# A third buffer for a head's queries and keys, for the first nine of 64 heads, in memory that the mixer's hidden tiles take later

## The chip, the cores and the metric

One core of a Trainium2 chip. The metric is the device time of one execution in microseconds (us); lower is better. The engines are TensorE (PE: matmuls, and PEld for its weight loads), VectorE (DVE), ScalarE (ACT), GpSimd (POOL) and SyncE (SP), which issues the transfers here. Each runs its own instructions in program order and waits for the others by semaphores.

## The reference, cut to what matters

Causal attention in blocks of 64 over 8 batches of 8 heads, 576 positions of 64 features each, then a mixer on the joined heads:

```python
scores = scale * np.matmul(q, k.transpose(0, 1, 3, 2))   # q, k, v: (8, 8, 576, 64)
scores = np.where(mask, scores, -1e9)                    # block_i >= block_j
attn = np.exp(scores - scores.max(-1, keepdims=True))
attn = attn / (attn.sum(-1, keepdims=True) + 1e-9)
out = np.matmul(attn, v)                                 # heads joined: x, (8, 576, 512)
u = x + ((x.transpose(0, 2, 1) @ U) @ V).transpose(0, 2, 1)
return u + np.maximum(u @ w_ch1, 0.0) @ w_ch2            # 512 -> 2048 -> 512
```

## The kernel before, in words

**Order of the work.** Nothing is written in program order. Each piece of work is added to a plan as a task: an engine, an estimated duration, a priority, the buffers it reads and writes. When all tasks are known, `issue` walks through the time that these estimates make and gives each engine, whenever it is idle there, the ready task with the lowest priority number whose PSUM banks are free. That walk fixes the order of the instructions on every engine; on the chip each engine keeps that order and waits where an estimate was off. So one changed dependency can move tasks on all engines, before and after the place itself.

**Heads.** Head `h` has priority `1000 * h` and a little. Its queries and keys are one transfer of 288 KB into a buffer `raw` (`split_qk`, issued at L886, or in two pieces at L889 for head 0): 64 partitions of features, 576 columns of queries, 576 of keys. The other 64 partitions hold constants that add the mask, filled once at the start (L828 to L836). ACT scales the keys in place (L902). `raw` is a ring of two, so head `h` takes `raw[h % 2]`, and its transfer has to wait until all the score products of head `h - 2` have read that buffer. The task of head `h + 1` has priority `1000 * h - 900`, ahead of the work of head `h`.

**Softmax of a head.** The 576 queries are five tiles. Tile 4 is the widest and has a double bank of its own (`bw`, only one); tile 3 takes one of two banks `bf` for heads below 8; tiles 2, and 1 with 0, take banks of the four `ba`, leaving at least one. The products are L962 in full fp32 for heads below 12 (L966 and L967 after that), DVE takes the maximum (L980), ACT the exponential (L991) into `p`, DVE and POOL normalise (L1007, L1008, L1017), PE transposes (L1050), ACT or DVE copies to `pw` for heads below 10 (L1027, L1025), PE multiplies by V (L1093). Every second head `mix` adds the low-rank part (L1134 to L1168) and stores `u` (L1173).

**Weights and mixer.** In the same stretch the mixer's first weights arrive as 64-bit words, 512 KB at a time (L372, L387), and are put together to fp32 by ACT and DVE (L353, L331, L332, L337, L345) and split in two parts (L360, L361). When the first block's eight heads are through and the first weights stand, mixer products (L465, L488) fill TensorE between the heads. After the attention, later weights and products in another scheme (L659) go on to the end.

**Memory.** The pool `ep` holds `pw`, which only heads below 10 use. Its room is given up by a task `hidden` once these heads are done, and taken over by `hh` and `hl`, the results of the ReLU.

Of the kernel before, what the change touches and what calls it, by code (L numbers as in the profile page):

```python
# [9 lines left out]
F32 = mybir.dt.float32  # L10
# [6 lines left out]
P = 128  # L17
S = 576
# [119 lines left out]
class Plan:  # L138
# [8 lines left out]
    def add(self, engine, ns, prio, fn, reads=(), writes=(), hold=(), after=0, port=False):  # L147

        n = len(self.tasks)
        deps = set()  # L150
        for b in reads:
            deps.update(b.writers)
            b.readers.append(n)
        for b in hold:
            deps.update(b.readers, b.writers)
        for b in writes:
            deps.update(b.readers, b.writers)
            b.writers, b.readers = [n], []
        deps.discard(n)
        slots = {b for b in (*reads, *writes) if b.pool is not None}  # L160
        for b in slots:
            b.users += 1
        self.tasks.append((engine, ns, prio, fn, deps, after, slots, port or engine == "POOL"))
# [76 lines left out]
def _act(n, sbuf=False):  # L240
    return (93 if sbuf else 52) + 0.833 * n


def _dve(n):
    return 69 + 1.042 * n


def _pe(*ns, m=()):

    m = [*m, *[P] * len(ns)][1 : len(ns)] + [P]  # L250
    return sum(max(0.85 * w, n * COL) for n, w in zip(ns, m))
# [3 lines left out]
def attention_then_mixer(  # L255
# [21 lines left out]
    def f32(ap):  # L277
        return ap.bitcast(F32)
# [6 lines left out]
    ap = actx.enter_context(tc.tile_pool(name="ap", bufs=1))  # L285
    ep = ectx.enter_context(tc.tile_pool(name="ep", bufs=1, side="right"))

    def buf(pool, shape, dtype, name):
        return Buf(pool.tile(shape, dtype, name=name))

    def ring(pool, n, shape, dtype, name):
        return [buf(pool, shape, dtype, f"{name}{i}") for i in range(n)]
# [500 lines left out]

    q2_r = ring(ap, 2, [P, S], F32R, "q2_")
    k2_r = ring(ap, 2, [P, S], F32R, "k2_")
    raw_r = ring(ap, 2, [P, 2 * S], F32, "raw")
    ss_r = [b.split(5) for b in ring(ap, 2, [P, 5, 2], F32, "ss")]

    pt_r = [ring(ap, PB[i], [P, P * (i + 1)], F32, f"p{i}_") for i in range(5)]
# [2 lines left out]
    def transposed(pool, dtype, name):  # L802
        return [
            buf(pool, [P, _at(g, NK[g] - 1).stop], dtype, f"{name}{g}").split(len(BLOCKS[g])) for g in range(2)
        ]

    pw_r = [transposed(ep, F32, f"pw{n}") for n in range(2)]
    q1_r = ring(ap, 2, [P, S], F32R, "q1_")
    k1_r = ring(ap, 2, [P, S], F32R, "k1_")
# [69 lines left out]
            )  # L879

    def split_qk(h, pr):
        raw, q1, k1, q2, k2 = (r[h % 2] for r in (raw_r, q1_r, k1_r, q2_r, k2_r))

        def fetch():
            if h:
                nc.sync.dma_start(out=raw[0:64, :], in_=qk[h])  # L886
            else:
                for a in (S, 0):
                    nc.sync.dma_start(out=raw[0:64, a : a + S], in_=qk[h, :, a : a + S])  # L889

        if h in (FS - 2, FS - 1):

            for n, (x, o) in enumerate(((q2, 0), (k2, S))):
                add(
                    "DVE", _dve(S) / 2, pr, lambda x=x, o=o: nc.vector.tensor_copy(x[64:P, :], raw[64:P, o : o + S]),
                    [raw], [x],
                )
        add("SP", 820, pr, fetch, writes=[raw], after=DL)
        if h < FS:
            add(  # L900
                "ACT", _act(S, True), pr,
                lambda: nc.scalar.activation(raw[0:64, S : 2 * S], raw[0:64, S : 2 * S], AF.Copy, scale=SCALE), [raw], [raw],  # L902
            )
            return
        top = slice(0, 64)
        add("ACT", _act(S, True), pr, lambda: nc.scalar.copy(q2[top], raw[top, 0:S]), [raw], [q2])
        add(
            "ACT", _act(S, True), pr,
            lambda: nc.scalar.activation(raw[top, S : 2 * S], raw[top, S : 2 * S], AF.Copy, scale=SCALE), [raw], [raw],
        )  # L910
        add("ACT", _act(S, True), pr, lambda: nc.scalar.copy(k1[top], raw[top, S : 2 * S]), [raw], [k1])
        add("POOL", 1380, pr, lambda: nc.gpsimd.tensor_sub(q1[top], raw[top, 0:S], f32(q2[top])), [raw, q2], [q1])  # L912
        add("POOL", 1380, pr, lambda: nc.gpsimd.tensor_sub(k2[top], raw[top, S : 2 * S], f32(k1[top])), [raw, k1], [k2])  # L913

        add("SP", 600, pr, lambda: nc.sync.dma_start(out=f32(q1[64:P]), in_=f32(q2[top])), [q2], [q1], after=DL)
        add("SP", 600, pr, lambda: nc.sync.dma_start(out=f32(k1[64:P]), in_=f32(k1[top])), [k1], [k1], after=DL)
# [20 lines left out]
    def softmax(h, tiles, pr):  # L937

        q1, k1, q2, k2, ss, mx = (r[h % 2] for r in (q1_r, k1_r, q2_r, k2_r, ss_r, mx_r))
        raw = raw_r[h % 2]  # L940
        wide = 4 in tiles
        bank = Buf(pool=banks_w if wide else banks_f if h < 8 and tiles[0] == 3 else Rest(banks_a))

        parts, at = [], 0
        for i in tiles:
            parts.append((i, at))
            at += P * i + 64

        def view(i, at):
            return bank[:, :, :T] if wide else bank[: P if i else 64, at : at + P * i + 64]  # L950

        def products():
            for i, at in parts:
                qs = slice(P * i + 64 - (P if i else 64), P * i + 64)
                for j in range(2 if wide else 1):
                    o = bank[:, j, :T] if wide else view(i, at)
                    ks = slice(j * T, j * T + T) if wide else slice(0, P * i + 64)
                    if h < FS:
                        if not i:

                            o, qs = bank[:, at : at + 64], slice(0, P)
                        nc.tensor.matmul(  # L962
                            o, raw[:, qs], raw[:, S + ks.start : S + ks.stop], start=True, stop=True
                        )
                        continue
                    nc.tensor.matmul(o, q1[:, qs], k1[:, ks], start=True, stop=False)  # L966
                    nc.tensor.matmul(o, q2[:, qs], k2[:, ks], start=False, stop=True)  # L967

        ns, ms = [], []
        for i in tiles:  # L970
            ns += [T] * 4 if wide else [P * i + 64] * 2
            ms += [P if i else 64] * (4 if wide else 2)
        if h < FS:
            add("PE", sum(1.667 * n for n in ns) / 2, pr, products, [raw], [bank])
        else:
            add("PE", _pe(*ns, m=ms), pr, products, [q1, k1, q2, k2], [bank])
        for i, at in parts:
            add(
                "DVE", _dve(P * i + 64), pr,
                lambda i=i, at=at: nc.vector.tensor_reduce(  # L980
                    out=mx[: P if i else 64, i : i + 1], in_=view(i, at), op=ALU.max, axis=AX.XY if wide else AX.X,
                    negate=True,
                ),
                [bank], [mx.parts[i]],
            )
        for i, at in parts:
            pt, rows = pt_r[i][h % PB[i]], P if i else 64

            def exponentials(i=i, at=at, pt=pt, rows=rows):
                out = pt[:rows, : P * i + 64]  # L990
                nc.scalar.activation(  # L991
                    out.rearrange("p (j k) -> p j k", j=2) if wide else out, view(i, at), AF.Exp,
                    bias=mx[:rows, i : i + 1], accum_out=ss[:rows, i, 0:1],
                )

            add(
                "ACT", _act(P * i + 64) + 188, pr, exponentials, [bank, *(mx.parts[i] for i in tiles)],
                [pt, ss.parts[i]],
            )
# [182 lines left out]

    wa = weight_tiles(wp, 0)
    split_qk(0, 0.0)
    split_v(0, 2.0)
    mixing_weights(MP)
# [32 lines left out]
            for n, b in enumerate(whole):  # L1219
                b.ap = t[:, 2 * n : 2 * n + 2, :]  # L1220

    early = [b for x in pw_r for y in x for b in y.parts]
    add("SP", 0, -1.0, hidden, early, hh_r + hl_r, hold=early)

    for n in range(2):
# [44 lines left out]
```

## Time and profile before

| | |
|---|---|
| median of 3 runs | 1182.55 us (1182.36 to 1183.16) |
| profiled execution | 1182.37 us, of which 1180.6 us are the profile's span |
| TensorE | busy 1164.1 us, 99% of the span |
| VectorE, ScalarE, GpSimd | 79%, 66%, 38% of the span |

The span starts with the first instruction of the profile and ends with the last; the 1.8 us around it are in the device time. A busy TensorE is a union of modelled instruction intervals, which overlap. A piece of the chain of work is the instruction that held up what came next.

### The profile page before, as it was taken

The page shows a single profiled execution, that of the slowest core. Times are in us where ns is not written, and L with a number is a line of the kernel's source. Part 1 is how long each engine was busy: PE and PEld are TensorE (multiplying, and loading weights), DVE is VectorE, ACT ScalarE, POOL GpSimd, SP SyncE. Part 2 cuts the span into 40 slices and gives each one's busy share as a digit, 9 for nine tenths or more (in the row PEclk, how much of TensorE's full clock was granted, in tenths as well). Part 3 has the DMA queues.
Part 4 walks back from the last instruction along what each step waited for, and adds up shares of the span by engine and source line. Part 5 has one row for each costly group of instructions (what it writes and reads, how often), then busy time and mean ns, then how long its engine had stood idle before and what let it go on. Part 6 is the DMA issues. An engine that isn't in the chain of part 4 may idle for free.

```text
span 1180.6 us, 25204 instructions
## 1 busy us (share of the span) xinstructions
PE 1164.1 (99%) x8988; PEld 1131.4 (96%) x8988; DVE 936.2 (79%) x2009; ACT 774.9 (66%) x1924; POOL 451.2 (38%) x582
## 2 busy tenths in 40 slices
PE   9989999999999999999999999999999999999998
PEld 7778999999999999999999999999999999999998
DVE  6898887877887877777877587327989889889887
ACT  7888888989888888898887342114544444444443
POOL 5556876676757666766674122110000000000000
PEclk9999999999999999999999999999999999999999
DMA  4445565433433433443331434211132132132121
GB/s 142 141 153 154 160 177 140 116 115 108 114 112 110 123 105 111 114 117 110 112 94 52 142 113 145 66 52 50 61 122 71 51 121 70 53 121 62 60 81 41
DMA packets 75884, 122.69 MB, mean 104 GB/s; under 512 B 8944, under 2 KB 52976, under 8 KB 75760
## 3 DMA queue, kind: packets, MB, share of 16 engines
q1 hardware_dynamic: 75760, 121.09, 34.8%
q8 instruction: 71, 1.16, 0.4%
q14 instruction: 53, 0.43, 0.1%
HBM read 76.23 MB, written 29.49 MB: 90 GB/s over the span
## 4 chain that ended last, share of the span: by engine, by line
PE 81%; DVE 8%; ACT 7%; issue 2%; DMA 1%; SPq 0%; POOL 0%; ACTq 0%; DVEq 0%; POOLq 0%
PE bb L659 30%; PE bf L465 11%; PE bf L488 10%; PE ba L1050 7%; PE ba L1109 6%; PE bg L488 4%; PE bg L465 4%; ACT p L991 3%; DVE mx L980 2%; PE ba L967 2%; PE ba L966 2%; PE ba L1134 1%; PE bw L966 1%; PE ba L1148 1%; DVE pl L1069 1%
## 5 line engine op out<-in xcount | busy, mean ns | idle before, releaser
L1017 POOL TENSOR_SCALAR p<-p,rv 128x192 f32<-128x192 f32 (+4 forms) x320 | 171.8, 551 | 156.8 <-DVE rv L1008 85.2
L659 PE MATMUL bb<-hh,w1l 128*128 128x288 f32 x704 | 170.1, 295 | 0.0
L659 PE MATMUL bb<-hh,w1h 128*128 128x288 f32 x704 | 169.4, 295 | 0.0
L1069 DVE TENSOR_TENSOR pl<-ba,ph 128x512 fp32r<-128x512 f32 x216 | 113.7, 550 | 17.9 <-ACT ph L1027 15.7
L991 ACT ACTIVATE p<-ba,mx 128x448 f32<-128x448 f32 (+2 forms) x248 | 114.8, 466 | 16.4 <-DVE mx L980 12.8
L1050 PE MATMUL ba<-ident,p 128*128 128x128 f32 x768 | 122.8, 275 | 2.7 <-POOL p L1017 1.5
L659 PE MATMUL bb<-hl,w1h 128*128 128x288 f32 x576 | 123.0, 295 | 0.1
L659 PEld LDWEIGHTS bb<-hh,w1l 128*128 128x128 f32 x704 | 122.9, 190 | 0.0
L659 PEld LDWEIGHTS bb<-hh,w1h 128*128 128x128 f32 x704 | 121.9, 188 | 0.0
L488 PE MATMUL bf<-hh,w2h 128*128 128x288 f32 x384 | 118.8, 309 | 0.9 <-DVE hl L473 0.9
L488 PE MATMUL bf<-hl,w2h 128*128 128x288 f32 x384 | 113.5, 295 | 0.0
L488 PE MATMUL bf<-hh,w2l 128*128 128x288 f32 x384 | 112.7, 294 | 0.0
L447 POOL TENSOR_TENSOR ul<-ur,uh 128x288 fp32r<-128x288 f32 x72 | 61.5, 880 | 127.2 <-PE bf L465 80.9
L613 ACT CAST hh<-hb 128x576 fp32r<-128x576 f32 x98 | 65.9, 672 | 60.6 <-PE bb L659 59.3
L1027 ACT CAST ph<-ba 128x512 fp32r<-128x512 f32 x216 | 98.8, 491 | 9.1 <-PE ba L1050 7.8
L980 DVE TENSOR_REDUCE mx<-ba 128x1 f32<-128x448 f32 (+3 forms) x248 | 95.1, 406 | 10.1 <-PE ba L967 7.5
L1050 PEld LDWEIGHTS ba<-ident,p 128*128 128x128 f32 x768 | 89.9, 141 | 8.3 <-POOL p L1017 3.4
L659 PEld LDWEIGHTS bb<-hl,w1h 128*128 128x128 f32 x576 | 91.9, 188 | 0.4 <-DVE hl L614 0.4
L1109 PE MATMUL ba<-ph,vs 128*128 128x256 f32 (+3 forms) x432 | 89.9, 262 | 0.0
L465 PE MATMUL bf<-uh,w1l 128*128 128x288 f32 x392 | 82.1, 305 | 0.0
L913 POOL TENSOR_TENSOR k<-raw,k 64x576 fp32r<-64x576 f32 x52 | 75.1, 1444 | 2.1 <-POOL p L1017 0.5
L912 POOL TENSOR_TENSOR q<-raw,q 64x576 fp32r<-64x576 f32 x52 | 74.0, 1422 | 4.5 <-issue 2.1
(173 smaller groups left out, 3357.7 us busy)
## 6 DMA issues: line engine op xcount, KB each, us to landing
raw<-in_qk_dram SPq DMA_DIRECT2D x63, 288.0 KB, 3.9
st<-in_w_dram SPq DMA_DIRECT2D x32, 512.0 KB, 3.7
o_d<-ot SPq DMA_DIRECT2D x72, 144.0 KB, 1.8
vr<-in_v_dram SPq DMA_DIRECT2D x32, 320.0 KB, 3.7
ur<-u_d SPq DMA_DIRECT2D x64, 144.0 KB, 2.4
whole<-o_d SPq DMA_DIRECT2D x32, 288.0 KB, 3.1
out_dram<-whole SPq DMA_DIRECT2D x31, 288.0 KB, 2.2
ur<-u_d SPq DMA_DIRECT2D x30, 288.0 KB, 3.3
```

The costliest lines, as they stand in the source:

```text
L465: nc.tensor.matmul(ps[:, :T], w()[wn][:, k, fs], m[k].ap, start=(i == 0), stop=(i == len(ops) - 1))
L488: nc.tensor.matmul(ps[:, :T], w()[wn][:, f, ms], hs[f][x].ap, start=(i == 0), stop=(i == len(ops) - 1))
L659: nc.tensor.matmul(bank[:, i, :T], x()[:, w(k)], p.ap[:, k, :], start=first and n == 0, stop=last and n == len(ops) - 1)
L912: add("POOL", 1380, pr, lambda: nc.gpsimd.tensor_sub(q1[top], raw[top, 0:S], f32(q2[top])), [raw, q2], [q1])
L913: add("POOL", 1380, pr, lambda: nc.gpsimd.tensor_sub(k2[top], raw[top, S : 2 * S], f32(k1[top])), [raw, k1], [k2])
L980: lambda i=i, at=at: nc.vector.tensor_reduce(out=mx[: P if i else 64, i : i + 1], in_=view(i, at), op=ALU.max, axis=AX.XY if wide else AX. ...
L991: nc.scalar.activation(out.rearrange("p (j k) -> p j k", j=2) if wide else out, view(i, at), AF.Exp, bias=mx[:rows, i : i + 1], accum_out= ...
L1017: lambda x=x, rows=rows, i=i: nc.gpsimd.tensor_scalar(out=x, in0=x, scalar1=rv[:rows, i : i + 1], scalar2=1.0, op0=ALU.mult, op1=ALU.mult),
L1027: add("ACT", _act(n), pr, lambda: nc.scalar.copy(out(), inp()), reads, writes)
L1050: nc.tensor.transpose(out=bank[:, a : a + P], in_=pt_r[i][h % PB[i]][:, j * P : (j + 1) * P], identity=perm.ap)
L1069: "DVE", _dve(m), pr, lambda: nc.vector.tensor_sub(pl[:, low], bank[:, :m], f32(ph[:, low])), [bank, bh], [bl]
L1109: nc.tensor.matmul(bank[0 : c.stop, a:n], vs[:, j, c], x[:, _at(g, j)], start=(i == 0), stop=(i == len(ops) - 1))
```

## The change

Heads 0 to 8 rotate over three buffers instead of two (`h % 3`). From head 9 on the first two alternate again: head 9 takes buffer 0, head 10 buffer 1, and so on. The third buffer lies in the pool `ep`, beside `pw`; `hidden` waits for its readers too. The loop that fills the constants runs over the ring, so it fills a third buffer at the start. Its length, 4.6 KB in each partition, fits in the room that `hh` and `hl` take later, so nothing else shrinks.

```diff
-    raw_r = ring(ap, 2, [P, 2 * S], F32, "raw")
+
+    raw_r = ring(ap, 2, [P, 2 * S], F32, "raw") + ring(ep, 1, [P, 2 * S], F32, "rawe")
+
+    def raw_of(h):
+        return raw_r[h % 3 if h < 9 else (h + 1) % 2]
+
...
     def split_qk(h, pr):
-        raw, q1, k1, q2, k2 = (r[h % 2] for r in (raw_r, q1_r, k1_r, q2_r, k2_r))
+        q1, k1, q2, k2 = (r[h % 2] for r in (q1_r, k1_r, q2_r, k2_r))
+        raw = raw_of(h)
...
     def softmax(h, tiles, pr):
...
-        raw = raw_r[h % 2]
+        raw = raw_of(h)
...
-    early = [b for x in pw_r for y in x for b in y.parts]
+    early = [raw_r[2], *(b for x in pw_r for y in x for b in y.parts)]
     add("SP", 0, -1.0, hidden, early, hh_r + hl_r, hold=early)
```

## Rows read from the trace of the kernel before

**Rows 1.** The page: busy time and share of the span, by engine.
```profile
PE 1164.1 (99%) x8988; PEld 1131.4 (96%) x8988; DVE 936.2 (79%) x2009; ACT 774.9 (66%) x1924; POOL 451.2 (38%) x582
```

**Rows 2.** Busy time of the engines in stretches, PEclk the granted clock's share.
```profile
core 0: us, PE busy (x) PEld busy (x) DVE busy (x) ACT busy (x) POOL busy (x), PEclk, DMA share, GB/s
0.00:100.00 100.00, 91.13 (x529) 74.23 (x529) 82.74 (x214) 80.91 (x225) 57.09 (x85) 1.00 0.46 142
100.00:200.00 100.00, 97.94 (x783) 93.98 (x783) 86.34 (x213) 85.82 (x237) 74.77 (x90) 1.00 0.58 165
200.00:300.00 100.00, 99.57 (x827) 96.67 (x826) 79.77 (x218) 89.13 (x253) 67.50 (x87) 1.00 0.40 112
```

**Rows 3.** The same for tens of us within the first hundred.
```profile
60.00:70.00 10.00, 8.93 (x61) 7.48 (x60) 9.24 (x21) 7.87 (x20) 5.61 (x7) 1.00 0.59 189
70.00:80.00 10.00, 9.00 (x51) 6.98 (x49) 9.73 (x20) 8.25 (x24) 3.99 (x6) 1.00 0.30 107
80.00:90.00 10.00, 8.90 (x56) 6.58 (x54) 9.76 (x23) 8.07 (x22) 6.12 (x8) 1.00 0.51 147
90.00:100.00 10.00, 9.25 (x55) 7.80 (x55) 7.73 (x19) 8.03 (x25) 7.89 (x10) 1.00 0.40 134
```

**Rows 4.** Whom TensorE waited for, first 200 us, the two longest in total.
```profile
PE bw L962 <- ACT raw L902: 2.3, 2, 1.2
PE ba L1050 <- POOL p L1017: 1.5, 2, 0.8
```

**Rows 5.** SP's transfers in order of time (start, duration of the issue).
```profile
1.99 0.59 SPq L886 DMA_DIRECT2D raw<-in_qk_dram  x1
2.63 0.60 SPq L925 DMA_DIRECT2D vr<-in_v_dram  x1
3.27 0.43 SPq L852 DMA_DIRECT2D st<-in_U_dram  x1
...
8.29 0.47 SPq L886 DMA_DIRECT2D raw<-in_qk_dram  x1
...
28.84 0.47 SPq L886 DMA_DIRECT2D raw<-in_qk_dram  x1
...
42.66 0.47 SPq L886 DMA_DIRECT2D raw<-in_qk_dram  x1
```

**Rows 6.** ACT's timeline (idle time before and its cause in brackets).
```profile
7.52 0.32 ACT L353 ACTIVATE z<-st 128x128 f32<-128x128 f32 x1 [0.64 <-DMA st<-in_U_dram]
...
13.26 0.19 ACT L991 ACTIVATION_READ_ACCUMULATOR p<-bw,mx 128x1 f32 x1
13.35 0.67 ACT L902 ACTIVATE raw<-raw 64x576 f32<-64x576 f32 x1
...
43.81 0.20 ACT L991 ACTIVATION_READ_ACCUMULATOR p<-bw,mx 128x1 f32 x1
...
48.78 0.68 ACT L902 ACTIVATE raw<-raw 64x576 f32<-64x576 f32 x1 [1.51 <-DMA raw<-in_qk_dram]
```

**Rows 7.** TensorE's timeline: tile 4 of heads 2 and 6, and the first mixer product.
```profile
14.08 1.24 PE L962 MATMUL bw<-raw 128*128 128x288 f32 x4 [1.09 <-ACT raw L902]
...
49.52 1.24 PE L962 MATMUL bw<-raw 128*128 128x288 f32 x4 [1.19 <-ACT raw L902]
...
99.95 0.77 PE L465 MATMUL bf<-uh,w1h 128*128 128x288 f32 x4
```

**Rows 8.** The chain of work, 42 to 62 us.
```profile
42.13 0.50 PE ba L962 x4
...
42.66 6.10 DMA raw<-in_qk_dram
...
48.78 0.69 ACT raw L902
```

**Rows 9.** POOL's timeline at the start.
```profile
3.20 1.06 POOL L829 MEMSET raw<- 64x1152 f32 x1
4.33 0.79 POOL L833 TENSOR_SCALAR_AFFINE_SELECT raw<-raw 64x256 f32<-64x256 f32 x2
10.37 1.36 POOL L1017 TENSOR_SCALAR p<-p,rv 128x576 f32<-128x576 f32 x2 [5.25 <-DVE z L345]
```

**Rows 10.** DVE's groups of maxima in the first 100 us: tiles 2 to 0, 4, 3 (busy, mean ns).
```profile
L980 DVE TENSOR_REDUCE mx<-ba 128x1 f32<-128x320 f32 (+3 forms) x34 | 11.4, 373 | 0.9 <-PE ba L962 0.9
...
L980 DVE TENSOR_REDUCE mx<-bw 128x1 f32<-128x576 f32 x12 | 9.0, 749 | 6.2 <-PE bw L962 6.2
L980 DVE TENSOR_REDUCE mx<-bf 128x1 f32<-128x448 f32 x8 | 4.9, 612 | 0.6 <-PE bf L962 0.6
```

**Rows 11.** The page's transfers: KB of each and median us from issue to landing.
```profile
raw<-in_qk_dram SPq DMA_DIRECT2D x63, 288.0 KB, 3.9
```

## The prediction, made before the changed kernel ran

> **What bounds the kernel now.** First the page: TensorE is busy 1164.1 of 1180.6 us [rows 1], so 16.5 us without a matmul is all that any change in order can win; the matmuls themselves stay. Next the stretches, to see where those 16.5 us lie. The first 100 us hold 100 - 91.13 = 8.9 us, the second 2.1, the third 0.4 [rows 2]. The granted clock is full in all of them, so no part of the sum is a clock. The change acts on heads 0 to 9, which are through by about 100 us, when the first mixer product starts [rows 7]. It works exactly where TensorE still waits.
>
> Third, whom it waits for there. The longest entry is the one that this change is about: the products of tile 4 waited twice, 2.3 us together, for ACT's scaling of `raw` [rows 4]. The timeline places them: 1.09 us ahead of head 2 at 14.08 us, and 1.19 us ahead of head 6 at 49.52 us [rows 7].
>
> Fourth, what stood behind these. The chain of work from 42 us on reads: the last score products of head 4 end, the transfer into the buffer that they freed takes 6.10 us, then the scaling, then tile 4 [rows 8]. The transfer was issued at 42.66 us [rows 5], and ACT sat idle 1.51 us for it [rows 6]. So this is a buffer that came free too late. At head 2 it is half that: its transfer went out at 8.29 us [rows 5], and the scaling stood on ACT behind the exponential of head 1's tile 4, at 13.35 us [rows 6].
>
> The other gaps between 60 and 100 us sum to 1.07 + 1.00 + 1.10 + 0.75 = 3.9 us [rows 3]. There DVE is nearly full for three tens (9.24, 9.73, 9.76), with ACT at about 8 [rows 3]. A buffer does nothing about a full DVE.
>
> **The change part by part.**
>
> *The release.* With three buffers, the transfer of head h waits for head h - 3 instead of h - 2. Head 6 then waits for head 3, whose last products had been read by the time that head 5's transfer went out, at 28.84 us [rows 5]. Even with the 6.10 us that it took [rows 8] it would be there before 36 us and scaled before 37. What is late next is the double bank `bw`: it has to be read by the exponential of head 5, which ends at 43.81 + 0.20 = 44.0 us [rows 6]. That is 5.5 us ahead of 49.52, so the 1.19 us go. On ACT the 1.51 us go too, and from 48.78 us the chain runs on through ACT. Bounds for this place: 0, if what follows on DVE refills it, and 1.5, ACT's own idle time. I take 1.2, since both engines gain at least that.
>
> *Head 2.* Its transfer needs no release at all and goes out among the first. The bank is then the next thing late: head 1's exponential ends at 13.45 us [rows 6], 0.63 us ahead of 14.08. Tile 3 and the narrow tiles have other banks and may step in ahead. Bounds 0.6 to 1.1; I take 0.85.
>
> *The rest to 100 us.* Heads 7 to 10 also find their queries and keys earlier, so that the planner has one more head to choose from. Of the 3.9 us of gaps [rows 3], little waits for `raw` itself; the gaps wait for exponentials and normalisation, which start earlier if the scores do. Bounds: 0 and 3.9. I take a quarter, 1.0, as DVE is nearer to full than to idle there.
>
> *Added work.* POOL fills a third buffer: 1.06 + 0.79 = 1.85 us [rows 9]. It has 5.25 us idle right behind the second fill [rows 9]; nothing else is queued there, so it costs nothing. Without that cover the normalisation at 10.37 us, and the transposes behind it, would be 1.85 us late. Nothing reads the third buffer's constants before head 2.
>
> *Moved transfers.* SP carries one more 288 KB transfer ahead of the load of U, at 0.6 us an issue [rows 5], and the data engines another 288 KB, whose usual time to landing is 3.9 us [rows 11]. U was on time with ACT waiting 0.64 us for it, at 7.52 us, in front of the first exponential [rows 6]. So U may hold up ACT's queue: bounds 0 and, if a whole transfer's time stood ahead of U, 3.9. The transfers overlap and the planner can place U's task behind an exponential; nearest is one issue slot, 0.6, half of it hidden: 0.3. Later transfers of `raw` only move ahead in SP's order, each keeping its slot.
>
> From head 9 on the ring is two deep as before; head 9 takes the buffer of head 6, long read. `hidden` waits for head 8's scores, but head 9's `pw` is read later still, so it waits no longer. Cost nothing in either place, and if it did wait, ReLU results would be late at the first mixer products.
>
> *Sum:* 1.2 + 0.85 + 1.0 - 0.3 = 2.75 us. The profiled execution took 1182.37 us, its span and 1.77 around it: 1182.37 - 2.75 = 1179.6. The median is 0.18 above that execution, so **1179.8 us**, 0.23% less. What a measurement of this kernel can tell from no change is about 0.2%, 2.4 us, so this stands hardly beyond it.
>
> A rule weighed here: TensorE's busy time is not a measure of the room left, the weight loads' share is (the Trainium skill, Perfetto Trace Analysis, Identifying the Most-Contended Engine). By it the first 100 us, at 74.23 against 93.98 in the next hundred [rows 2], would have 19.8 us of room, and all of it won would mean 1162.8 us. The trace speaks against it in this stretch: four full-fp32 products of 288 columns take 1.24 us and four of the mixer's 0.77 [rows 7], so that weight loads are sparser even where TensorE has no gap. I go by the gaps.
>
> **The rivals.**
>
> *No change to be told, 0.33.* The wait is removed, but DVE and ACT set when 100 us is reached: they carry the same work, and what they gain at 49 us they lose behind the weights' tasks at 60 to 90 us [rows 3]. Then only the start stays, 0.85 - 0.3: 1182.0 us. For it: DVE's 97% there. Against it: DVE is busy 82.74 of the first 100 us [rows 2], so it is not a bound over the stretch.
>
> *Slower, 0.17.* A ready `raw` lets the planner place the next head's maxima ahead of the weights' tasks on DVE. One head has three in `ba`, 3 x 0.37, one in `bw`, 0.75, and one in `bf`, 0.61: 2.5 us [rows 10]. If the last weights of the first half come that much later, the first mixer product moves from 99.95 [rows 7] to about 102.4, and TensorE, out of heads whose tiles fit in the banks, waits. With 0.3 for U and no gain: 1182.55 + 2.8 = 1185.3 us. It decides when the first mixer product comes after 102 us. For it: DVE is fullest just there. Against it: the weights have priorities of their own, and the heads' work has to be done before the first mixer product in any order.
>
> *More than forecast, 0.08.* All gaps of 60 to 100 us go, with both waits: 3.9 + 1.09 + 1.19 = 6.2, which gives 1176.4 us. For it: most of these gaps wait for one head's chain of steps, and a second head in hand covers that. Against it: DVE. (The rule's 1162.8 has 0.01 of this, at most.)
>
> **How the numbers follow.** The forecast's mechanism has what is left, 0.42; its own range is 1178.0 to 1180.5. Nearly all of it lies beyond 0.2%: 0.40 with 0.02 on the other side. Faster: 0.40 + 0.08 = 0.48. Same: 0.33 + 0.02 = 0.35. Slower 0.17. The range reaches from a little beyond the third rival to the slower one's time, 1175.8 to 1185.3; what is left out is the half of that rival that costs more, and a small part of the third.
>
> **What would show it.** Right: no wait of TensorE or ACT for the scaling or for a transfer into `raw` behind 14 us; the transfer of head 6 issued near 30 us; tile 4 of head 6 at 44 to 46 us instead of 49.5; TensorE's gaps in the first 100 us down from 8.9 to about 6, the first mixer product at some 97 us, and the stretches after 200 us as they were. POOL's third fill ends by 7.2 us, and the normalisation still starts near 10.4. Wrong: the same sum of gaps with other names on them (DVE's weights, exponentials), a first mixer product at or behind 100 us, or ACT held by U in front of the first exponential by more than 1 us. As the order is planned anew, small waits far behind 100 us may come or go for no reason in the change; if the first 100 us gain what is said and the time does not, they are where to look.

## The result: 0.5% slower, though the first 100 us came out as forecast

The changed kernel takes 1188.60 us, the median of 4 executions (1187.47 to 1188.74), beside 1182.45 us for the kernel before on the same chip (1181.61 to 1183.16). The ratio is 1.005, 95% interval 1.0033 to 1.0068. The forecast was 1179.8 us, so the sign was wrong. The kernel before has slower executions too, mostly with a mean granted clock of 0.997 to 0.999 instead of 1.00, and on the chips of e5 to e8 and of e15 and e16 they were so many that its median there was 1183.8 and 1184.0 us, so that ratios from these two chips are some 0.1% lower than they would be beside 1182.5.

These are the page and the windows of the profile after, with columns as in [rows 1, 2]:

```profile
PE 1163.6 (98%) x8988; PEld 1133.8 (96%) x8988; DVE 939.7 (79%) x2009; ACT 775.4 (65%) x1924; POOL 452.5 (38%) x585
```
```profile
0.00:100.00 100.00, 93.65 (x551) 76.57 (x552) 79.43 (x219) 84.03 (x236) 60.60 (x90) 1.00 0.46 143
100.00:200.00 100.00, 88.33 (x689) 85.64 (x689) 85.99 (x190) 74.63 (x201) 64.74 (x76) 0.97 0.51 145
200.00:300.00 100.00, 99.38 (x827) 97.54 (x826) 78.04 (x212) 87.00 (x247) 68.01 (x88) 1.00 0.42 118
...
128.00:132.00 4.00, 1.52 (x8) 1.51 (x9) 3.93 (x8) 0.26 (x1) 2.17 (x2) 0.84 0.60 162
132.00:136.00 4.00, 4.00 (x33) 3.98 (x32) 2.77 (x6) 2.54 (x7) 0.00 (x0) 0.73 0.05 20
...
148.00:152.00 4.00, 4.00 (x21) 3.99 (x20) 2.60 (x6) 2.41 (x4) 4.00 (x5) 0.60 0.00 0
```

TensorE's gaps in the first 100 us went from 8.87 to 6.35 us, a gain of 2.5. In the second 100 us they went from 2.06 to 11.67, a loss of 9.6. The rest of the span has 5.2 us of gaps, 5.6 before. That is 6.7 us more gap, and TensorE's busy sum is 0.5 us less: together the 6.2 us by which the span grew (1180.6 to 1186.8). At 200 us TensorE had started 1240 matmuls, 1312 before. The granted clock, full in every stretch before, is 0.73 and 0.60 in two stretches of 4 us in which TensorE works without a gap, each time behind a long wait. These cost an estimated (0.27 + 0.40) x 4 = 2.7 us of TensorE's rate. They lie inside its busy time, whose ends are modelled, so that they can't be split off from the sum above.

**First 100 us.** Timelines of SP, ACT, POOL and TensorE in the profile after:

```profile
3.26 0.47 SPq L892 DMA_DIRECT2D rawe<-in_qk_dram  x1
...
29.26 0.47 SPq L892 DMA_DIRECT2D raw<-in_qk_dram  x1
...
8.59 0.68 ACT L908 ACTIVATE rawe<-rawe 64x576 f32<-64x576 f32 x1 [1.72 <-DMA rawe<-in_qk_dram]
9.18 0.72 ACT L997 ACTIVATE p<-bw,mx 128x576 f32<-128x576 f32 x1
...
6.19 0.78 POOL L838 TENSOR_SCALAR_AFFINE_SELECT rawe<-rawe 64x256 f32<-64x256 f32 x2
...
10.04 1.24 PE L968 MATMUL bw<-raw 128*128 128x288 f32 x4 [1.55 <-ACT p L997]
...
13.94 1.14 PE L968 MATMUL bw<-rawe 128*128 128x288 f32 x4
...
39.98 1.14 PE L968 MATMUL bw<-raw 128*128 128x288 f32 x4
...
94.75 0.77 PE L465 MATMUL bf<-uh,w1h 128*128 128x288 f32 x4
```

Heads 2 and 6 (13.94 and 39.98 us) have no wait in brackets any more; in [rows 7] they had 1.09 and 1.19. Head 6 is 9.5 us earlier, the first mixer product 5.2 us. Head 0's first exponential (L997, 9.18 us) is later than in the kernel before:

```profile
7.75 0.72 ACT L991 ACTIVATE p<-bw,mx 128x576 f32<-128x576 f32 x1
```

**Second 100 us.** Whom TensorE waited for in the first 200 us, the three longest; columns as in [rows 4]:

```profile
PE ba L1140 <- DVE xl L1145: 4.7, 2, 3.2
PE bf L488 <- DVE hl L473: 4.5, 2, 3.5
PE ba L1056 <- DVE pl L1075: 2.4, 3, 1.8
```

The wait for `raw`, the first of [rows 4], has gone from the list, and VectorE has taken its place. The timelines show four of the waits behind VectorE, with its passes ahead of them, and for the two longest GpSimd's work too:

```profile
99.41 2.45 DVE L331 TENSOR_SCALAR z<-z 128x512 f32<-128x512 f32 x1 [0.18 <-ACT z L353]
...
125.22 2.83 DVE L331 TENSOR_SCALAR z<-z 128x512 f32<-128x512 f32 x1 [1.26 <-ACT z L353]
128.09 1.37 DVE L332 TENSOR_SCALAR z<-z 128x512 int32<-128x512 int32 x1
129.38 0.44 DVE L473 SCALAR_TENSOR_TENSOR hl<-bf,hh 128x288 fp32r<-128x288 f32 x1
129.74 0.68 DVE L1145 TENSOR_TENSOR xl<-ba,xh 128x512 fp32r<-128x512 f32 x1
...
142.91 3.03 DVE L331 TENSOR_SCALAR z<-z 128x512 f32<-128x512 f32 x1
...
159.65 2.29 DVE L331 TENSOR_SCALAR z<-z 128x512 f32<-128x512 f32 x1
...
124.98 1.41 POOL L918 TENSOR_TENSOR q<-raw,q 64x576 fp32r<-64x576 f32 x1
126.36 1.41 POOL L919 TENSOR_TENSOR k<-raw,k 64x576 fp32r<-64x576 f32 x1
127.74 1.43 POOL L361 TENSOR_TENSOR w2l<-z,w2h 128x512 fp32r<-128x512 f32 x1
129.14 1.04 POOL L941 TENSOR_TENSOR vs<-vr,vs 128x320 fp32r<-128x320 f32 x1
...
142.62 3.05 POOL L447 TENSOR_TENSOR ul<-ur,uh 128x288 fp32r<-128x288 f32 x4
145.65 1.54 POOL L1023 TENSOR_SCALAR p<-p,rv 128x320 f32<-128x320 f32 x3
...
103.23 0.30 PE L1140 MATMUL ba<-ident,xt 128*64 128x128 f32 x1 [1.52 <-DVE xl L1145]
...
130.47 0.30 PE L1140 MATMUL ba<-ident,xt 128*64 128x128 f32 x1 [3.19 <-DVE xl L1145]
...
147.04 0.40 PE L488 MATMUL bf<-hh,w2h 128*128 128x288 f32 x1 [3.52 <-DVE hl L473]
...
163.68 0.52 PE L1056 MATMUL ba<-ident,p 128*128 128x128 f32 x3 [1.82 <-DVE pl L1075]
```

L331 (the clip) and L332 (the shift) work on a later weight in place, from memory to memory. Such a pass takes 0.42 us when nothing is beside it; at the two longest waits it takes 2.83, 1.37 and 3.03 us, and it ends a little behind the end of a GpSimd instruction (145.94 behind 145.65). `hl` and `xl`, which TensorE needs at once, stand behind it on VectorE. What the passes took beyond 0.42 us each is at least as long as TensorE's wait behind them at 103, 130 and 164 us, and 2.61 of the 3.52 us at 147 us. Summed, that is an estimated 1.52 + 3.19 + 2.61 + 1.82 = 9.1 of the 11.67 us of gaps, if nothing else had come late in place of the passes; the experiments show that often something does. VectorE's instructions that read PSUM are not stretched: `hl` takes 0.44 us beside GpSimd's 1.04. Between 100 and 180 us the groups read, before and after:

```profile
L331 DVE TENSOR_SCALAR z<-z 128x512 f32<-128x512 f32 x6 | 4.2, 702 | 0.0
```
```profile
L331 DVE TENSOR_SCALAR z<-z 128x512 f32<-128x512 f32 x7 | 11.9, 1694 | 1.9 <-ACT z L353 1.9
```

GpSimd's run of four is no novelty. The kernel before has the same run from 126.77 us on, but then VectorE has `pl`, `hl` and `xl` to do, which read PSUM, and its clip comes behind the run:

```profile
133.40 0.43 DVE L331 TENSOR_SCALAR z<-z 128x512 f32<-128x512 f32 x1
```

What the new order changed is what stands beside the run. The Trainium skill (SBUF — State Buffer, section SBUF: two separate sides) calls the ports that VectorE and GpSimd share an exclusive lock, held for a whole instruction; these rows agree that a pass is blocked outright, with 2.83 and 3.03 us for 0.42, but they were held through the ends of two and of four instructions of GpSimd, not of one.

The planner knows of such meetings. In `issue`, a task marked `port`, as these passes are, is not started while a GpSimd task runs, nor the other way round (`not (port and tasks[n][7])`). In the planned time they never meet. Where they meet on the chip, the engines are not where the estimates put them.

### The profile page after: what moved, and what is told of

Its sections match the earlier page's. It is cut to its first block, busy times and chain, and to the rows that moved or that the text cites. A ratio compares the mean times of both kernels' runs of the same rounds, so it can differ in the third digit from the quotient of the medians.

```text
span 1186.8 us, 25168 instructions
## 1 busy us (share of the span) xinstructions
PE 1163.6 (98%) x8988; PEld 1133.8 (96%) x8988; DVE 939.7 (79%) x2009; ACT 775.4 (65%) x1924; POOL 452.5 (38%) x585
## 4 chain that ended last, share of the span: by engine, by line
PE 79%; DVE 6%; ACT 6%; issue 2%; DMA 0%; POOL 0%; ACTq 0%; DVEq 0%; POOLq 0%
PE bb L659 30%; PE bf L488 11%; PE bf L465 11%; PE ba L1056 6%; PE ba L1115 6%; PE bg L488 4%; PE bg L465 4%; ACT p L997 2%; PE ba L973 2%; PE ba L972 2%; DVE mx L986 1%; PE ba L1154 1%; DVE z L331 1%; PE ba L1140 1%; PE bw L972 1%
## 5 line engine op out<-in xcount | busy, mean ns | idle before, releaser
L997 ACT ACTIVATE p<-ba,mx 128x448 f32<-128x448 f32 (+3 forms) x248 | 114.6, 465 | 10.7 <-DVE mx L986 6.4
L465 PE MATMUL bf<-uh,w1l 128*128 128x288 f32 x408 | 86.2, 306 | 0.0
L488 PEld LDWEIGHTS bf<-hh,w2h 128*128 128x128 f32 x384 | 72.9, 190 | 5.1 <-DVE hl L473 5.0
L1123 DVE TENSOR_TENSOR xt<-ba,tmp 64x256 f32<-64x256 f32 x108 | 48.0, 448 | 35.7 <-ACT tmp L1121 34.0
```

Source lines behind the costliest of these rows:

```text
L465: nc.tensor.matmul(ps[:, :T], w()[wn][:, k, fs], m[k].ap, start=(i == 0), stop=(i == len(ops) - 1))
L488: nc.tensor.matmul(ps[:, :T], w()[wn][:, f, ms], hs[f][x].ap, start=(i == 0), stop=(i == len(ops) - 1))
L997: nc.scalar.activation(out.rearrange("p (j k) -> p j k", j=2) if wide else out, view(i, at), AF.Exp, bias=mx[:rows, i : i + 1], accum_out= ...
```

## The experiments

There are five theories. **A**: passes that GpSimd holds up cost the time. **B**: the new order is late by itself, whatever is held. **C**: the buffer's fill, its transfers or its releases cost it. **D**: any order planned anew is a draw, this one a bad one. **E**: a third buffer makes any order worse. Ratios are to the kernel before on the same chip, with 95% intervals. The table has TensorE's busy time of the first and second 100 us, the lowest granted clock in a stretch of 4 us (multiples of 4) among the first 200, and the longest of VectorE's passes from memory to memory there, in us (undisturbed they take 0.28 to 0.67). The ratio is that of the medians; the other columns are those of one profiled execution.

| kernel | ratio | 0 to 100 | 100 to 200 | clock | longest pass |
|---|---|---|---|---|---|
| before | 1 | 91.13 | 97.94 | 1.00 | 2.23 |
| after | 1.005 | 93.65 | 88.33 | 0.60 | 3.03 |
| e4 fill and room only | 0.9991 | 90.84 | 97.78 | 1.00 | 2.24 |
| e3 third buffer, order of before | 1.0002 | 91.95 | 97.86 | 1.00 | 2.23 |
| e6, e5 shorter GpSimd work, before and after | 0.9979, 1.001 | 91.77, 94.26 | 98.01, 91.82 | 1.00, 0.57 | 2.24, 2.70 |
| e2, e1 strided passes, before and after | 0.9997, 1.0053 | 91.91, 93.92 | 97.74, 89.83 | 1.00, 0.57 | 2.25, 2.84 |
| e14, e13 passes through `y`, before and after | 1.0026, 1.0062 | 90.75, 92.35 | 94.98, 92.23 | 0.59, 0.60 | 3.17, 3.38 |
| e16, e15 the last five of them only | 1.0021, 1.0027 | 91.03, 93.69 | 96.09, 90.68 | 0.76, 0.57 | 3.17, 4.63 |
| e7, e8 estimate 175, before and after | 1.0052, 1.0073 | 91.52, 94.08 | 93.09, 89.44 | 0.73, 0.58 | 3.91, 3.25 |
| e12, e11 estimate 155, before and after | 0.9988, 1.0051 | 91.82, 94.99 | 97.84, 90.69 | 1.00, 0.50 | 2.24, 5.02 |
| e18 estimate 150, before | 1.0028 | 91.95 | 96.06 | 0.57 | 3.46 |
| e9, e10 three buffers for six, three heads | 1.0028, 1.0056 | 93.05, 91.24 | 89.14, 93.04 | 0.63, 0.75 | 2.89, 3.32 |
| e17 third buffer in the order of e12 | 0.9987 | 90.74 | 96.05 | 0.59 | 3.17 |

The last column divides the profiles as the clock does: at most 2.25 us where the clock is full in the first 200 us, and 2.70 to 5.02 us in the other fourteen. That fits A; alone it doesn't show which of the two comes first.

**The buffer without the new order: e4 and e3.** e4 allocates and fills the third buffer and never uses it. e3 uses it on the chip, but shows the planner two, so that every engine keeps the order of before.

```diff
 def raw_of(h):
-    return raw_r[h % 3 if h < 9 else (h + 1) % 2]
+    return raw_r[h % 2]                                                  # e4
+    return raw_q[h % 2], raw_r[h % 3 if h < 9 else (h + 1) % 2]          # e3: plan raw_q, run raw_r
```

> The changed kernel with the third buffer allocated and filled but never used: every head takes h % 2, the order is that of before. What the fill and the room cost by themselves. All theories: 1182 to 1183.5 us; above 1184 the fill on GpSimd or the moved addresses cost something.

> The changed kernel with its three buffers, but planned with the two-buffer dependencies, so that every engine keeps the order of the kernel before (GpSimd has the third fill besides). Only the release on the chip is earlier. Theory A (the loss is the new order's, not the buffer's): 1179 to 1183 us, no hole above 1.5 us behind 100 us, the wait of 1.19 us ahead of head 6 shrinks if the transfer's place in SP's queue lets it go out earlier. Theory C (an earlier release costs by itself, by transfers that meet or by banks): 1185 to 1189 us.

e4: 0.9991 (0.9979 to 1.0004), e3: 1.0002 (0.9988 to 1.0015). Fill, room and releases cost nothing that can be told: C falls. In e3 the wait ahead of head 6 is shorter but not gone, 0.67 us for 1.19 in [rows 7], since SP's transfer keeps its place in the order:

```profile
48.86 1.24 PE L970 MATMUL bw<-raw 128*128 128x288 f32 x4 [0.67 <-ACT raw L910]
```

So the buffer alone is worth about nothing: its gain and the loss both need the new order.

**Less work on GpSimd: e5 (changed kernel) and e6 (kernel before).** Three of GpSimd's instructions are cut short (two of them shown), so that part of the low-order correction is left out. The order stays as it was in each.

```diff
-        add("POOL", 1380, pr, lambda: nc.gpsimd.tensor_sub(q1[top], raw[top, 0:S], f32(q2[top])), [raw, q2], [q1])
+        add("POOL", 1380, pr, lambda n=S if h < 14 else D: nc.gpsimd.tensor_sub(q1[top, 0:n], raw[top, 0:n], f32(q2[top, 0:n])), [raw, q2], [q1])
...
-                "POOL", 780, E, lambda u=ur[k], h=uh, l=ul: nc.gpsimd.tensor_sub(l.ap, u.ap, f32(h.ap)),
+                "POOL", 780, E, lambda u=ur[k], h=uh, l=ul, n=R if c or turn else T: nc.gpsimd.tensor_sub(l[:, 0:n], u[:, 0:n], f32(h[:, 0:n])),
```

> The changed kernel, same order on every engine, with three of GpSimd's instructions cut short: the low parts of queries and keys from head 14 on (64 of 576 columns instead of all) and the low parts of the mixer's input from the second chunk on (32 of 288 columns). Part of the low-order correction is left out. Theory A (VectorE's clip pass is held by GpSimd instructions that follow each other without a pause): the passes at 125, 143 and 160 us fall from 2.8, 3.0 and 2.3 us to below 1, TensorE's holes of 3.2, 3.5 and 1.8 us behind them go; the pass at 99 us, which stands beside other GpSimd work (the weights' and V's low parts), keeps its 2.4 us and its hole of 1.5; clock back at full; 1178 to 1182 us. Theory B (late by the order itself): the holes stay, 1186 us or more.

> The kernel before with the same three instructions cut short. Control: theory A has little to win here, no hole above 1 us stands behind 20 us in it: 1180.5 to 1182.8 us. If this gains as much as the changed kernel does, the shortened work is the gain and not the meeting.

e5 1.001 (0.9999 to 1.0021), e6 0.9979 (0.997 to 0.9988): the difference shrinks from 0.50% to 0.31%, by 0.19%, while the intervals of the ratios together allow 0.23% either way; so no share of the loss is measured here. By the expectations 1184.39 us lies between A and B. Where GpSimd's run is broken up, the pass isn't held and TensorE's gap behind it falls from 3.52 to 0.82 us. VectorE and GpSimd in e5, at the place of 142.91 in the profile after:

```profile
143.90 0.41 DVE L331 TENSOR_SCALAR z<-z 128x512 f32<-128x512 f32 x1
...
142.88 0.51 POOL L447 TENSOR_TENSOR ul<-ur,uh 128x32 fp32r<-128x32 f32 x2 [0.35 <-PE bf L465]
144.34 0.75 POOL L447 TENSOR_TENSOR ul<-ur,uh 128x32 fp32r<-128x32 f32 x2 [0.95 <-ACT uh L445]
```

Of the three passes that A expected below 1 us, this is the only one: the other two still take 2.70 and 2.01 us, beside work that was not shortened, and two more, at 99.73 and 120.23 us, take 2.45 and 2.41. TensorE's waits behind the first three of these are 2.10, 0.99 and 1.52 us. So the rows show A at one place, and the time doesn't show how much of the loss it is. The edit also gives GpSimd's results earlier, from which the control gains too. The rest can be B, or what is still held.

**Every second word: e1 (changed) and e2 (before).** An attempt to take the passes out of the lock.

```diff
+            w = z.rearrange("p (a b) -> p b a", b=2)
-            nc.vector.tensor_scalar(out=f32(z), in0=f32(z), scalar1=MOST, scalar2=LEAST, op0=ALU.min, op1=ALU.max)
+            nc.vector.tensor_scalar(out=f32(w), in0=f32(w), scalar1=MOST, scalar2=LEAST, op0=ALU.min, op1=ALU.max)
...
-                out=z, in0=z, scalar1=3, scalar2=0x3FFFFFFF, op0=ALU.logical_shift_left, op1=ALU.bitwise_and
+                out=w, in0=w, scalar1=3, scalar2=0x3FFFFFFF, op0=ALU.logical_shift_left, op1=ALU.bitwise_and
```

> The changed kernel with one edit: the two shift passes over a weight's words (clip, shift and mask) go through the same words in another sequence, every second word first, so that both passes see a step of two; same values, same order of instructions on every engine. Theory A (the new order puts these passes beside back-to-back GpSimd work, and VectorE is held until GpSimd pauses): the clip pass, 1.69 us on average from 100 to 180 us, falls to 0.6 to 0.8 with none above 1.3; TensorE's three holes of 1.8 to 3.5 us at 130, 147 and 164 us go, and its clock stays at full; 1177 to 1182 us. Theory B (the heads run ahead and the weights or the ReLU's low halves are late by the order itself): the holes stay and the time is 1186 to 1190 us, or a little more, as the passes are longer without company.

> The kernel before with the same edit of the two passes. Theory A: before had few such collisions (the clip took 0.70 us on average from 100 to 180 us, with single ones of 2.25 at 76 us), so it gains little: 1179 to 1183 us. Theory B: the passes only get longer, nothing else: 1182 to 1185 us.

e1 1.0053 (1.0038 to 1.0067), e2 0.9997 (0.9985 to 1.0009). The edit failed at what it was for: the passes were held as before, 1.38 us in the mean between 100 and 180 us, one of them 2.84. By its expectation 1189.74 us would be B's, but as the passes stayed held, the run tells nothing between the theories.

**Source and target of unlike shape: e13 and e14 for all 16 early pieces, e15 and e16 for the last five.** The clip goes from `z` to a spare buffer `y`, the shift back from `y` to `z`: 7 rows of 73 words against a run of 511, and the 9 words left over apart (the views are written in words here).

```diff
+    y = buf(ap, [P, 2 * T], I32, "y")
...
+            cuts = [(z, z)]
+            if n == CW and not whole:      # e15, e16: and used["shift"] > 11
+                cuts = [(z[:, 503:512] as 3 x 3, y[:, 525:537] as 3 rows of 4, 3 of each), (z[:, 0:511] as 7 x 73, y[:, 0:525] as 7 rows of 75, 73 of each)]
+            for a, b in cuts: nc.vector.tensor_scalar(out=f32(b), in0=f32(a), scalar1=MOST, scalar2=LEAST, op0=ALU.min, op1=ALU.max)
+            for a, b in cuts: nc.vector.tensor_scalar(out=a, in0=b, scalar1=3, scalar2=0x3FFFFFFF, op0=ALU.logical_shift_left, op1=ALU.bitwise_and)
```

> The changed kernel, same order on every engine, with the two shift passes of the early weights sent through a spare buffer whose rows are 7 runs of 73 words, not one of 511 (and 9 words apart from them), so that source and target of a pass differ in shape and the passes run a word at a time, 0.55 to 0.65 us each instead of 0.42, plus 0.06 us for the 9 words. If that takes them off the way that they share with GpSimd: theory A (the loss is VectorE held by GpSimd in these passes) expects no pass above 1 us, the holes at 130, 147 and 164 us gone and 1179 to 1183 us, in spite of some 0.5 us more VectorE time a weight. Theory B (late by the order itself): passes short, holes still there, 1186 us or more. If the passes are still held for 2 to 3 us, the edit did not take them off and the run tells nothing.

> The kernel before with the same passes through the spare buffer. Control: its passes were seldom held, so it loses a little of VectorE's time or nothing: 1181 to 1185 us. If it gains as much as the changed kernel, the meetings are no matter of the change.

> The changed kernel with only the last five of the sixteen early weights' passes, those from 99 us on, sent through the spare buffer, word by word, so that the first 95 us are as in the changed kernel. Theory A (held passes): first 100 us as in the changed kernel, waits of TensorE from 100 to 200 us down from 11.6 us to 3 or less, clock full, 1178 to 1182 us. Theory B (late by the order, whichever instruction is held): waits there come to 6 us or more under other names, with the clock below full after the longest, 1184 to 1189 us.

> The kernel before with the passes of its last five early weights word by word. Control: none of its passes there was held for more than 1.7 us, so 1181.5 to 1184 us by either theory.

e13 1.0062 (1.0047 to 1.0077), e14 1.0026 (1.0015 to 1.0037). The clip and the shift are not held at all now; the two groups that use `y` in e13 (duration in ns: least, median, most):

```profile
L335 DVE TENSOR_SCALAR y<-z x32: 142/414/677, 30.2 to 161.5; 128x9 f32<-128x9 f32 x16, 128x511 f32<-128x511 f32 x16
L336 DVE TENSOR_SCALAR z<-y x32: 161/424/686, 31.0 to 162.4; 128x9 int32<-128x9 int32 x16, 128x511 int32<-128x511 int32 x16
```

None is over 0.69 us. Yet e13 comes out at 1190.06 us, which its expectation gave to B, and the difference to the control is still 0.36%. That doesn't settle it for B, because the holding moved to the next pass that works from memory to memory, with a wait of TensorE of 1.87 us behind it:

```profile
147.22 3.38 DVE L339 SCALAR_TENSOR_TENSOR z<-st,z 128x512 int32<-128x512 int32 x1
```

Besides, 16 pieces take four instructions for two, and VectorE has this in the first 100 us as well: TensorE's gain there halves (92.35 for 93.65). The control loses 0.26%, more than was expected (1185.72 us for 1181 to 1185); there, too, such a pass (L347) is held for 3.17 us, with a wait of 2.36 us behind it. e15 and e16 change only the passes behind 99 us: 1.0027 (1.0017 to 1.0036) beside 1.0021 (1.0009 to 1.0032). The difference between changed and unchanged kernel falls from 0.50% to 0.06%, but half of that is the control's own loss (1186.2 us, expected 1181.5 to 1184), with L348 held for 3.17 us in it. In e15 the gaps at 130 us (0.63 for 3.19) and 147 us (1.64 for 3.52) shrink, and here, too, the holding moves to the next pass that reads and writes memory alone, L340, which takes 0.67 us when it is free. VectorE, GpSimd and TensorE in e15:

```profile
142.77 4.63 DVE L340 SCALAR_TENSOR_TENSOR z<-st,z 128x512 int32<-128x512 int32 x1
...
139.94 3.08 POOL L450 TENSOR_TENSOR ul<-ur,uh 128x288 fp32r<-128x288 f32 x4
143.00 1.22 POOL L1026 TENSOR_SCALAR p<-p,rv 128x320 f32<-128x320 f32 x3
144.20 1.42 POOL L922 TENSOR_TENSOR k<-raw,k 64x576 fp32r<-64x576 f32 x1
145.59 1.26 POOL L364 TENSOR_TENSOR w2l<-z,w2h 128x512 fp32r<-128x512 f32 x1
...
148.60 0.61 PE L491 MATMUL bf<-hh,w2h 128*128 128x288 f32 x1 [3.11 <-DVE ot L497]
```

The pass waits until GpSimd pauses at 146.85 us, TensorE waits 3.11 us for what stands behind it, and the granted clock of the 4 us behind is 0.57. By its expectation e15 is B's outcome: 9.3 us of gaps and 1187.2 us, where A wanted 3 us or less and 1178 to 1182. The rows show A's mechanism a second time, at another instruction. An edit of one kind of pass moves the holding and doesn't end it, so that none of these runs parts A from B.

**The order drawn anew, with two buffers and with three: e7, e8, e11, e12, e18.** One estimate of the planner moves by 10 or 15 ns; no work changes.

```diff
-TAIL = {"PE": 165, "DVE": 78, "ACT": 105, "POOL": 20, "SP": 0}
+TAIL = {"PE": 175, "DVE": 78, "ACT": 105, "POOL": 20, "SP": 0}    # e7 before, e8 after; 155: e12, e11; 150: e18 before
```

> The kernel before, two buffers, with one estimate of the planner changed: what it adds behind a TensorE task before others may use its result, 175 ns instead of 165. No instruction changes, only the order. Theory D (the loss is where the planner's order happens to put VectorE's passes against GpSimd): other orders without the buffer move by some us too, 1180 to 1190 us. Theory E (the third buffer makes it worse in any order, heads too far ahead): this stays at 1181.5 to 1183.5 us.

> The changed kernel with the same estimate at 175 ns. Theory D: the first 100 us keep their gain of some 2.5 us without the collisions at 130 and 147 us, or others come: anywhere from 1178 to 1190 us. Theory E: 1186 us or more, with holes of 2 us and more from 100 to 180 us again.

> The kernel before with the same estimate at 155 ns. Theory D: 1180 to 1190 us, a spread over orders as wide as the change's loss. Theory E: 1181.5 to 1183.5 us.

> The changed kernel with the planner's estimate behind a TensorE task at 155 ns instead of 165: another order again. Theory D: 1178 to 1190 us, the loss not tied to the buffer. Theory E: 1186 us or more.

> Two buffers; only the estimate of TensorE's tail is 150 ns instead of 165, so the order is drawn once more. By D (each new order is a draw, and 165 and 155 ns were two good ones, 175 ns a bad one) anything from 0.998 to 1.006 with about even chances of either side of 1.001, and over 1.002 only with VectorE's passes of the weights held by GpSimd in the profile and a stretch of granted clock near 0.6. By E (only orders with the buffer planned in are bad, 175 ns was the exception) 0.998 to 1.001, and full clock.

With two buffers: e7 1.0052 (1.0036 to 1.0067), e12 0.9988 (0.9979 to 0.9997), e18 1.0028 (1.0019 to 1.0037). With the change: e8 1.0073 (1.0056 to 1.009), e11 1.0051 (1.0036 to 1.0066). e7 loses all that the change lost, without a third buffer. In e7 and e18 a pass beside GpSimd's run is held up to 3.91 and 3.46 us, with TensorE's gaps of 2.64 and 2.06 us behind it. e18's VectorE and GpSimd:

```profile
125.81 3.46 DVE L345 SCALAR_TENSOR_TENSOR z<-st,z 128x512 int32<-128x512 int32 x1
...
125.95 1.40 POOL L912 TENSOR_TENSOR q<-raw,q 64x576 fp32r<-64x576 f32 x1
127.31 1.41 POOL L913 TENSOR_TENSOR k<-raw,k 64x576 fp32r<-64x576 f32 x1
```

So an order can be this bad without the buffer: D holds at least in part, and E's expectations for e7, e12 and e18 failed. e8 is even slower (1191.86 us) than D's range allowed. e11 has the best first 100 us of all (94.99) and is as slow as the change.

**Fewer heads on three buffers: e9 and e10.**

```diff
-        return raw_r[h % 3 if h < 9 else (h + 1) % 2]
+        return raw_r[h % 3 if h < 6 else h % 2]            # e9
+        return raw_r[h % 3 if h < 3 else (h + 1) % 2]      # e10
```

> The third buffer for the first six heads only (heads 6 and on alternate over the first two). Theory D (luck of the order): the gain of the first 50 us stays, 1 to 2 us, and what the order does behind 100 us is another draw: 1178 to 1190 us. Theory E (heads too far ahead at 100 us): with the lead given back before the mixer starts, 1180 to 1182.5 us.

> The third buffer for the first three heads only: the transfer of head 2 goes out at the start, all later heads alternate. Theory D: gain of the start 0.6 to 1.1 us and another draw behind: 1178 to 1190 us. Theory E: 1181 to 1182.5 us.

1.0028 (1.0016 to 1.004) and 1.0056 (1.0041 to 1.0071): no dose and response. Three heads cost as much as nine, six perhaps less. Both lie in D's range, which was wide, and beyond E's.

**The third buffer in the better order: e17.** As e3, with the estimate of e12.

```diff
+TAIL = {"PE": 155, "DVE": 78, "ACT": 105, "POOL": 20, "SP": 0}
...
+    return raw_q[h % 2], raw_r[h % 3 if h < 9 else (h + 1) % 2]
```

> Three buffers, rotated as in the change, but with the order in which the two-buffer kernel with the estimate of 155 ns runs on every engine (that kernel measured 0.9988 of the kernel before). If the loss is in the order alone (theories B and D), the third buffer takes TensorE's wait ahead of head 6 down by about 0.5 us and nothing else, as it did in the old order: 0.9975 to 0.999, 1179.5 to 1181.3 us, and the best of all so far with the reference's full work. If the third buffer costs something in any order (C, E), 1.002 or more, 1184.9 us and up. The granted clock is full throughout by B and D, with no stretch of 4 us below 0.9.

0.9987 (0.9978 to 0.9996), 1180.93 us: the best beside e6, which leaves work out, but not to be told from e12, so again the buffer brings nothing. Expected was a full clock; the profiled execution has two stretches near 0.6 all the same. It is the slowest of its 11 executions, which reach from 1178.96 to 1183.9 us, so this profile is not the typical one. Ahead of the second stretch TensorE waits 2.35 us for what stands behind L345, held for 3.17 us there; in e12, with the same order, the same pass took 1.66. An order alone doesn't fix whether a pass is held.

**What stays open.** All five orders planned with the buffer were slower, by 0.28 to 0.73%; of four with two buffers (165, 175, 155 and 150 ns) two were. That is too few to tell E from D. One argument for E is that starting mixer work 5 us earlier brings more weights' passes beside GpSimd's work. The traces speak against it: e8 and e10 have the buffer and start their first mixer product at 100.37 and 100.74 us, as late as the kernel before (99.95), and are no faster than the change; e7, without the buffer, starts it at 101.05. No run has the changed order without held passes, so B is neither shown nor ruled out.

## Why the prediction was wrong, step by step

- *Release of head 6:* right. Its transfer goes out at 29.26 us (forecast: near 30), tile 4 runs at 39.98 with no wait (forecast: 44 to 46), and ACT's wait for the transfer is gone.
- *Head 2:* half right. The wait of 1.09 us went, but tile 4 moved only from 14.08 to 13.94. ACT runs head 2's scaling ahead of head 0's first exponential and waits 1.72 us for the transfer there. The exponential starts at 9.18 instead of 7.75 us, and head 1's tile 4 waits 1.55 us for the bank. TensorE's first ten us have 7.46 us of work for 8.95, the next ten 9.96 for 8.15: a gain of 0.3, where 0.85 - 0.3 was summed. The loss was looked for at U, which the planner moved out of the way.
- *POOL's fill:* right, it ends at 6.97 us (forecast: by 7.2). The normalisation starts 0.8 us later than in [rows 9], because the exponentials do.
- *The sum for the first 100 us:* right within its bounds, 2.5 us for 2.75, but not term by term. Between 40 and 60 us, where head 6 stood, TensorE gained 0.7 us where 1.2 was summed; between 20 and 40 us it gained 0.4, for which there was no term; from 60 to 100 us it gained 1.1 where 1.0 was summed. That the total fits so well is partly luck. The first mixer product came at 94.75 (forecast: 97), where the slower rival had put it at 102.4; its mechanism did not happen, though its time was the nearest.
- *The step that failed* is the sum's end at 100 us. Behind it the prediction expected only that "small waits far behind 100 us may come or go for no reason in the change", and put them at nothing, though it named them as the place to look if the time did not follow the first 100 us. The change acts on heads 0 to 9, but the planner orders all behind them anew from the new state. That order costs 9.6 us of gaps between 100 and 200 us, and the clock behind two of them. The sum had no term for it and the range no room: before, this stretch had 2.1 us of gaps [rows 2], so a loss there was unlimited above and a gain at most 2.1. This asymmetry stood in the rows.
- *What the runs put in its place:* fill and releases cost nothing (e3, e4); VectorE's passes beside GpSimd's runs are held, and TensorE waits behind them (shown by the rows of the profile after, e5 and e15; by those rows an estimated 9.1 of the 11.67 us of gaps stand behind held passes); the same loss comes from 10 ns in an estimate (e7). That the order costs it is shown by e3. How much would be left of it without held passes is not settled, as no edit took them all away.

## What to carry to other kernels

Where an order is planned, a change of a buffer is two changes: run it once in the old order (e3) to price the buffer, and price the new order by several draws, since 10 ns in one estimate moved this kernel by -0.12% or +0.52%. Look at the stretch that is nearly full, not only at the one with gaps: it has much to lose and little to win. Where VectorE's memory-to-memory passes are queued ahead of something that TensorE needs soon, see what GpSimd does in those microseconds.

## What was not expected of the hardware

- VectorE's passes from memory to memory wait for more than the GpSimd instruction at hand: 4.63 us for a pass of 0.67, which ended only 0.55 us after GpSimd, at work without a pause since 139.94, had stopped at 146.85 (e15). Reading every second word changed nothing (e1); passes with unlike shapes of source and target took 0.67 and 0.69 us in the mean (clip and shift, 511 words) instead of 0.42 and were never held (e13).
- The granted clock read 0.50 to 0.81 in single stretches of 4 us behind waits of TensorE, the lowest of them (0.50, e11) at the lower of its two levels, 1.2 GHz. Somewhat over half of these waits were of 2 to 3.6 us, but shorter ones did it too: 1.52 us in e5 (0.57), and two of 0.59 and 1.21 us in e13, where four products of tile 4 took 2.29 us instead of 1.24. A wait of the same length does not always do it: the same 1.52 us in the profile after brought no fall, nor did 2.10 us in e5. Of the kernels profiled, the six with a full clock in the first 200 us lie at 0.9979 to 1.0002; of the fourteen others all but e17 at 1.001 to 1.0073. Why the waits of the first 100 us before, 8.9 us in all, brought no such fall in its profile is open.
